# RWKV-5 attention followed by top-1 expert routing: own weights as column tiles, a scaling table held in PSUM, weights and routing steps moved

## The chip, the cores and the metric

The kernel runs on one core of one Trainium2 chip. The metric is the device time of one execution in microseconds (us). A core has five engines that run side by side and meet by semaphores: TensorE (PE; its weight loads are listed as PEld), VectorE (DVE), ScalarE (ACT), GpSimd (POOL) and SyncE (SP), which here only issues transfers. Transfers run on 16 DMA engines that the core's queues share.

## The reference

Two blocks follow each other. The first is RWKV-5 attention over r, k, v of batch 4, 8 heads, 768 steps and head size 48, with a decay w and a bonus u for each head and channel:

```python
for t in range(S):
    cur = np.einsum('bhd,bhe->bhde', u[None] * kt, vt)
    y[:, :, t] = np.einsum('bhd,bhde->bhe', rt, state + cur)
    state = w[None, :, :, None] * state + np.einsum('bhd,bhe->bhde', kt, vt)
```

Its output, 3072 tokens of 384 values, is the input of the second block, a switch layer with 8 experts of hidden size 1024. Each token goes to the expert with the largest logit:

```python
logits = x @ w_gate
expert_idx = np.argmax(logits, axis=1)
h = np.maximum(xe @ w1[e], 0.0)      # xe: the tokens of expert e
out[mask] = gate_w[mask, None] * (h @ w2[e])
```

All is float32. The step of u, by which a token weighs its own value, is a sum over 48 channels of r * k * u: one number for each token and head. It is called "own weight" below.

## The kernel before

The input decides between a path for usual decays, `fast()`, and a general one. These inputs take `fast()`, whose order of instructions on every engine is written out by hand (`manual_schedule`); nothing is planned by a scheduler there. Waits between engines are added by the framework.

**Attention: 32 units.** A unit is one batch, one half of the sequence (384 steps, 3 chunks of 128) and one pair of heads (hp, 0 to 3). The two heads of a pair lie on partitions 0 to 47 and 64 to 111; rows 48 to 63 and 112 to 127 of r and k are zero. Units run in the order batch, half, pair. For a unit:

- `load_rk`, `load_kt` and `load_v` bring r and k (two halves of 144 KB), k with tokens on partitions, and v (144 KB each). SP issues them five units ahead. SP's transfers take turns on eight semaphores, so each waits for the landing of the eighth before it.
- `u_scale_k` (POOL) makes RK = r * k (L518) and K = k * W2 (L519); `u_scale_r` (DVE) makes R = r * W1 (L514); `u_scale_g` (POOL) makes Kg (L524). W1 and W2 are tables of powers of w, one row of 128 for each pair, made by ACT with `scaled` (L468). The first two units are scaled on DVE by `u_scale_first`.
- `u_own` (L536) multiplies RK by u: for each chunk and head one matmul of 48 rows and 128 columns, with one result column, written behind the scores in the PSUM bank of that head (P0 or P1). `u_products` (L546) makes the scores, 128 by 128 for each chunk and head, in the same banks.
- `u_diagonal` (ACT) copies the own weights out as dv (L554) and writes them on the diagonal of A (L557). `u_mask` (DVE, L568) copies the scores below the diagonal over it.
- `u_state` sums k and v of each chunk on PE in the bank Gp (L582) and runs the state over the chunks on DVE (L587, L589).
- `u_out` multiplies the old state by R (L603) and v by A (L607), for one head in each half of the columns of the array, into one of two banks yp, which ACT copies out as y (L610).

In step u of the loop the engines get: the loads of unit u+5; the scalings of u+2; scores, state and mask of u+1; `u_out(u)`. Every fourth step aside, `u_gate` (L638) then turns a finished chunk of 128 tokens to rows and makes its 8 logits. PSUM has eight banks: two each for P0, P1 and y, one for Gp, one for gates.

**Weights.** `pieces` cuts the weights that the first experts need into transfers of 384 KB: w2 of experts 0 to 4 (`w2_load`, NW = 5), and w1 of the first two expert tiles. Three are issued before the loop; the others are spread over the steps that have no row stores. The w2 of experts 5 to 7 lies where attention keeps its own buffers, and is loaded as these come free.

**Routing.** For each batch, small DVE and ACT steps (`choose`) take the maximum, the chosen expert and its weight; `ranks` counts tokens for each expert with matmuls into a y bank, and `onehots` (L851) makes one-hot matrices of the ranks. The list `todo` spreads these steps and the stores of rows (L196) over the loop; what belongs to the fourth batch comes after it. `Routes.early` makes the lists of tokens of the first two expert tiles from the first two batches; `to_index` (L861 to L872) turns one-hot products into token indices.

**Experts.** 24 tiles of 128 tokens follow, then a tile of short segments that is woven in: `hidden` (L1078) multiplies w1 by the tokens, `product` (L1089) multiplies by w2, `weigh` and `store` write rows back. Tiles 0 and 1 use what was prepared early, so the last routing steps run on DVE beside them: `ranks`, `bases`, `order`, `slots`, `onehots`, and `index`, whose matmuls (L861) stand inside `t1.hidden`. Only then are the experts of tiles 2 and later known, and SP loads their w1 (L1031).

Of the kernel before, what the change touches and what calls it, by code (L numbers as in the profile page):

```python
# [10 lines left out]
FP32 = mybir.dt.float32  # L11
# [37 lines left out]
def bc(ap, shape):  # L49
    return ap.to_broadcast(shape)  # L50
# [3 lines left out]
def rwkv5_then_switch(ctx, tc, r, k, v, rk, tok, wu_in, wg, wgh, w1, w2, out):  # L54
# [18 lines left out]
    wu = consts.tile([128, 2, HP], FP32, name="wu")  # L73
# [156 lines left out]
    def general():  # L230
# [24 lines left out]

        ub = ca.tile([128, HP, 2], FP32, name="ub")
        nc.vector.memset(ub, 0.0)
        for hi in range(2):
            q = slice(64 * hi, 64 * hi + 64)
            nc.vector.tensor_copy(ub[q, :, hi], wu[q, 1, :])  # L260
# [39 lines left out]
        def half(b, hp, hf, kT, rT, vt, St, xb):  # L300
# [41 lines left out]
            for c in range(HC):  # L342
                if c < ns:
                    nc.tensor.matmul(dsp[:, c * 2 * D:(c + 1) * 2 * D], lhsT=Kt[:, c, :], rhs=vt[:, c0 + c, :],
                                     start=True, stop=True, skip_group_check=True)
                nc.tensor.matmul(dsp[:, nd + 2 * c:nd + 2 * c + 2], lhsT=RK[:, c * C:(c + 1) * C],
                                 rhs=ub[:, hp, :], start=True, stop=True, skip_group_check=True)
# [81 lines left out]
    def fast():  # L429
# [12 lines left out]
        with tc.manual_schedule():  # L442
            nc.gpsimd.tensor_tensor(RKs[0], rks[0][:, 0:HC * C], rks[0][:, HC * C:], op=ALU.mult)

# [13 lines left out]
        Gp = ps.tile([128, HC, 2, 64], FP32, name="Gp", tag="g", bufs=1)  # L458


        W1 = ca.tile([128, HP, C], FP32, name="W1")
# [8 lines left out]
        def tables(hp):  # L470
            scaled(W2, Wr, hp, w_64)
            scaled(W1, Wp, hp, w_64)

# [5 lines left out]

        def idle(n):  # L480

            warm = ps.tile([128, 128], FP32, name="warm", tag="y", bufs=2)
            for i in range(n):
                nc.tensor.matmul(warm, lhsT=ident, rhs=ident, start=True, stop=True, skip_group_check=True)
# [17 lines left out]
        def u_scale_first(u):  # L502

            x = units[u]
            hp = x["hp"]
            if u:
                nc.vector.tensor_tensor(x["RK"], x["r"], x["k"], op=ALU.mult)
            for o, i, tab in (("K", "k", Wr), ("R", "r", Wp)):
                nc.vector.scalar_tensor_tensor(out=x[o], in0=x[i], scalar=w_64[:, hp:hp + 1],
                                               in1=bc(tab[:, hp, None, :], [128, HC, C]), op0=ALU.mult, op1=ALU.mult)  # L510

        def u_scale_r(u):
            x = units[u]
            nc.vector.tensor_tensor(x["R"], x["r"], bc(W1[:, x["hp"], None, :], [128, HC, C]), op=ALU.mult)  # L514

        def u_scale_k(u):
            x = units[u]
            nc.gpsimd.tensor_tensor(x["RK"], x["r"], x["k"], op=ALU.mult)  # L518
            nc.gpsimd.tensor_tensor(x["K"], x["k"], bc(W2[:, x["hp"], None, :], [128, HC, C]), op=ALU.mult)  # L519
# [8 lines left out]
        def u_own(u):  # L528

            x = units[u]  # L530
            hp, P = x["hp"], x["P"]
            for c in range(HC):
                for hi in range(2):
                    q = slice(64 * hi, 64 * hi + D)
                    o = HC * C + c
                    nc.tensor.matmul(P[hi][:, o:o + 1], lhsT=x["RK"][q, c, :],  # L536
                                     rhs=wu[q, 1, hp:hp + 1], start=True, stop=True, skip_group_check=True)
# [11 lines left out]
        def u_diagonal(u):  # L549
            x = units[u]  # L550
            A, P = x["A"], x["P"]
            dv = ca.tile([128, 2, HC], FP32, name="dv", bufs=2)
            for hi in range(2):
                nc.scalar.copy(dv[:, hi], P[hi][:, HC * C:HC * C + HC])  # L554
            for hi in range(2):
                for c in range(HC):
                    nc.scalar.activation(A[:, hi, c, :], ident, func=ACT.Copy, scale=dv[:, hi, c:c + 1])  # L557

        def u_scores(u, parts=(u_own, u_products, u_diagonal)):
            units[u]["P"] = [ps.tile([128, 512], FP32, name=f"P{hi}", tag=f"P{hi}", bufs=2) for hi in range(2)]  # L560
            for part in parts:
                part(u)
# [31 lines left out]
        def u_out(u):  # L594

            x = units[u]
            yp = ps.tile([128, HC, C], FP32, name="yp", tag="y", bufs=2)
            for c in range(HC):
                old = x["St"][:, c - 1] if c else units[u - HP]["St"][:, HC - 1] if x["hf"] else None
                for hi in range(2):  # L600
                    q = slice(64 * hi, 64 * hi + 64)
                    if old is not None:
                        nc.tensor.matmul(yp[q, c, :], lhsT=old[:, hi, :], rhs=x["R"][:, c, :],  # L603
                                         start=True, stop=False, skip_group_check=True)
                for hi in range(2):
                    q = slice(64 * hi, 64 * hi + 64)
                    nc.tensor.matmul(yp[q, c, :], lhsT=vh(x, c, hi, 64), rhs=x["A"][:, hi, c, :],  # L607
                                     start=old is None, stop=True, skip_group_check=True)
            x["y"] = cy.tile([128, HC * C], FP32, name="y", tag="y", bufs=8)
            nc.scalar.copy(x["y"], yp.rearrange("p c t -> p (c t)"))  # L610
# [40 lines left out]
        stores = set()  # L651
        for b in range(B - 1):
            g = 2 * HP * (b + 1) + 2
            for i in range(3):
                todo[g + min(i, 1)].append(lambda b=b, i=i: chosen[b][i]())
            for i in range(3):
                todo[g + 1 + i].append(lambda b=b, i=i: chosen[b][3](i, 3))
                stores.add(g + 1 + i)
            for i, step in enumerate(R.ranks(b, "y") + R.onehots(b, 3)):
                todo[min(g + 2 + max(i - 1, 0), NU - 1)].append(step)  # L660
            if b == NB - 1:
                for step, i in zip(R.early("y"), (5, 6, 8, 11)):
                    todo[g + i].append(step)
# [3 lines left out]
        pieces = [lambda e=e, i=i: w2_load(e, q=slice(i, i + 1)) for e in range(NW) for i in range(FQ)]  # L667
        n = FQ * (NW - 1)
# [6 lines left out]
        with tc.manual_schedule():  # L675
# [8 lines left out]
            u_scores(0, (u_own, u_diagonal, u_products))  # L684
            tables(2)
            u_scale_first(1)
# [3 lines left out]
            u_mask(0)  # L690
            u_scores(1, (u_own, u_diagonal, u_products))
            u_scale_g(0)
            load_kt(4)
            u_scale_g(1)
            for hp in (3, 0, 1):
                tables(hp)
            u_state(0)
            u_scale_r(2)
            idle(2)
            for u in range(NU):  # L700
# [6 lines left out]
                if u == NU - 1:  # L707
                    w2_load(NW)
                if u + 2 < NU:
                    u_scale_k(u + 2)  # L710
                    if u:
                        u_scale_r(u + 2)
                    u_scale_g(u + 2)
                if u == 0:
                    u_out(0)
                    u_mask(1)
                    u_state(1)
                elif u + 1 < NU:
                    u_scores(u + 1)
                    u_state(u + 1)  # L720
                    u_mask(u + 1)
                if u:
                    u_out(u)
                if u == 2:
                    gate_columns()
# [27 lines left out]
            w2_load(E - 1)  # L753
# [14 lines left out]
            t2.load_w1(wp, FQ)  # L768
            t0.weigh(mo)
# [15 lines left out]
    class Routes:  # L785
# [15 lines left out]

        def begin(self):
# [6 lines left out]
        def ranks(self, b, tag):  # L809
# [4 lines left out]
            def product():  # L814
                nonlocal rp
                rp = self.ps.tile([128, G + 1, E], FP32, name="rkp", tag=tag, bufs=BUFS[tag])
# [40 lines left out]
        def to_index(self, pool, Bv, n, n_chunks, tag, nm):  # L857

            idp = self.ps.tile([128, 2, n], FP32, name="idp", tag=tag, bufs=BUFS[tag])
            for g in range(n_chunks):  # L860
                nc.tensor.matmul(idp.rearrange("p u j -> p (u j)"), lhsT=self.At[:, g, :],  # L861
                                 rhs=Bv[:, g].rearrange("p u j -> p (u j)"), start=g == 0, stop=g == n_chunks - 1)
            idl = pool.tile([128, 2, n], FP32, name=nm + "l")
            nc.vector.tensor_copy(idl, idp)
            emp = pool.tile([128, n], FP32, name=nm + "e")
            nc.vector.tensor_scalar(out=emp, in0=idl[:, 0, :], scalar1=0.0, scalar2=float(N + 128),
                                    op0=ALU.is_equal, op1=ALU.mult)
            raw = pool.tile([128, n], FP32, name=nm + "r")
            nc.vector.scalar_tensor_tensor(out=raw, in0=idl[:, 0, :], scalar=128.0, in1=idl[:, 1, :],
# [402 lines left out]
def _layout(name, *a):  # L1272
# [10 lines left out]
    elif name == 'w,u':  # L1283
        q = _np.stack([x.reshape(HP, 2, D).transpose(1, 2, 0) for x in a], axis=2)
        q = _np.concatenate([q] + [q[:, D - 1:]] * (64 - D), axis=1)
        a = q.reshape(128, 2, HP)
    else:
        a = a[0]
# [34 lines left out]
```

## Time and profile before

| | |
|---|---|
| median of 3 runs | 411.44 us (410.87 to 412.72) |
| profiled execution, own time | 410.42 us |
| its span, first to last instruction | 408.7 us |
| granted TensorE clock, mean | 0.989 |
| busy: PE, DVE, POOL, ACT | 394.4, 241.7, 150.1, 127.6 us |
| moved by DMA | 99.01 MB, mean 242 GB/s |
| L536 own, 384 matmul records | 26.6 us busy, 250 ns each |
| L514 R, 30 | 21.3 us busy, 709 ns each |
| L518 RK, 30 | 31.8 us busy, 1060 ns each |

A matmul of float32 stands in the trace as two pairs of weight load and matmul, so the 192 instructions of `u_own` are 384 records. Matmuls are pipelined: the mean of one is longer than the time between two. How long a group holds PE is read from the chain of work that ended last, in order of time. Busy shares are means over stages with different limits. A wait is put down to the semaphore event that came last by the profile; where the named engine had long been done, it was another, often a transfer. The trace also has the landing of each transfer as events of its semaphore.

### The profile page before, as it was taken

The numbers are of one execution on the slowest core, as the hardware profiler recorded it, in microseconds if no ns is written. First come the engines' busy times: TensorE is split into PE (matmuls) and PEld (weight loads), VectorE is DVE, ScalarE is ACT, GpSimd is POOL, SyncE is SP. The second block draws the span as 40 slices with busy tenths as digits, with TensorE's granted clock in tenths as the row PEclk, the third lists the DMA queues.
The fourth block names the chain that finished last, engine by engine and source line by source line (L and its number), as shares of the span: only waits on it lengthen the run. The fifth ranks groups of instructions, "written<-read, shape, count | busy, mean of one in ns | idle before, by whom it ended". The sixth has DMA issues, their size and how long they took to land.

```text
span 408.7 us, 10600 instructions
## 1 busy us (share of the span) xinstructions
PE 394.4 (96%) x3983; PEld 325.2 (80%) x3983; DVE 241.7 (59%) x800; ACT 127.6 (31%) x395; POOL 150.1 (37%) x194
## 2 busy tenths in 40 slices
PE   7999999999999999999999999999999999999980
PEld 7899999999999777788878777777778787777760
DVE  7886688889986834444884574646444444343400
ACT  3787777787674221111111011011111110110110
POOL 6898779668770021121111222121222111110100
PEclk9999999999999999999999999999999999999995
DMA  7999999999999959569967696977868675555001
GB/s 257 268 281 267 257 277 304 267 270 303 287 259 374 297 153 377 193 200 337 327 223 244 203 337 213 321 226 246 305 214 285 230 269 194 178 189 174 34 24 27
DMA packets 42995, 99.01 MB, mean 242 GB/s; under 512 B 5237, under 2 KB 16522, under 8 KB 42930
## 3 DMA queue, kind: packets, MB, share of 16 engines
q1 hardware_dynamic: 39072, 86.94, 66.4%
q0 software_dynamic: 3712, 11.23, 9.0%
q8 instruction: 36, 0.59, 0.7%
q14 instruction: 29, 0.24, 0.2%
q10 hardware_dynamic: 146, 0.01, 0.0%
HBM read 88.72 MB, written 9.65 MB: 241 GB/s over the span
## 4 chain that ended last, share of the span: by engine, by line
PE 94%; DMA 1%; SPq 1%; ACT 1%; POOL 0%; issue 0%; DVE 0%; POOLq 0%
PE hp L1078 32%; PE yp L1089 30%; PE P L536 6%; PE P L546 6%; PE yp L607 5%; PE yp L603 4%; PE rp L638 4%; PE Gp L582 3%; PE hg L1138 1%; PE yg L1155 1%; DMA w_all<-in_r_k_units_dram 1%; ACT A L557 0%; PE idp L861 0%; PE xTp L1059 0%; SPq L96 0%; SPq L108 0%
## 5 line engine op out<-in xcount | busy, mean ns | idle before, releaser
L1078 PEld LDWEIGHTS hp<-xT,w1s 128*128 128x128 f32 x1152 | 133.1, 192 | 10.4 <-issue 3.7
L1078 PE MATMUL hp<-xT,w1s 128*128 128x128 f32 x1152 | 135.2, 276 | 0.0
L1089 PE MATMUL yp<-w_all,hT 128*128 (+1 forms) x384 | 128.0, 486 | 0.0
L1089 PEld LDWEIGHTS yp<-w_all,hT 128*128 128x128 f32 x384 | 71.1, 190 | 44.2
L1080 ACT ACTIVATE hT<-hp 128x512 f32<-128x512 f32 x48 | 28.7, 598 | 217.9 <-PE hp L1078 189.8
L1009 DVE STREAM_TRANSPOSE xT<-xs 32x96 f32<-32x96 f32 x336 | 90.4, 269 | 5.1 <-DMA xs<-x_hbm,idx 0.2
L1100 POOL DMA_INDIRECT out_dram<-yo,idx x22 | 22.3, 1013 | 183.8 <-DVE yo L1093 175.6
L1093 DVE TENSOR_SCALAR yo<-yp,xs 128x384 f32<-128x384 f32 x22 | 13.6, 618 | 114.0 <-PE yp L1089 114.0
L557 ACT ACTIVATE A<-ident,dv 128x128 f32<-128x128 f32 x192 | 59.7, 389 | 0.2 <-ACT dv L554 0.2
L568 DVE COPY_PREDICATED A<-mask,P 128x384 f32<-128x384 int32 x64 | 36.6, 589 | 7.0 <-ACT A L557 6.3
L518 POOL TENSOR_TENSOR w_all<-w_all 128x384 f32<-128x384 f32 x30 | 31.8, 1060 | 21.3 <-PE yp L607 7.2
L607 PE MATMUL yp<-A,w_all 128*64 128x128 f32 x384 | 38.2, 274 | 0.0
L1053 POOL DMA_INDIRECT xs<-x_hbm,idx x22 | 21.3, 969 | 31.1 <-DVE oe L967 24.7
L603 PE MATMUL yp<-w_all,St 128*64 128x128 f32 x320 | 31.7, 274 | 0.0
L519 POOL TENSOR_TENSOR w_all<-w_all,W 128x384 f32<-128x384 f32 x30 | 30.8, 1027 | 0.0
L546 PE MATMUL P<-w_all 48*128 48x128 f32 x384 | 29.5, 286 | 0.5 <-ACT dv L554 0.5
L536 PEld LDWEIGHTS P<-wu,w_all 48*128 48x128 f32 x384 | 23.9, 187 | 4.3 <-issue 1.4
L536 PE MATMUL P<-wu,w_all 48*128 48x1 f32 x384 | 26.6, 250 | 0.2 <-DMA w_all<-in_r_k_units_dram 0.2
L524 POOL TENSOR_TENSOR Kg<-w_all,Wg 128x288 f32<-128x288 f32 (+1 forms) x32 | 25.0, 784 | 2.3 <-DVE Wg L478 2.3
L546 PEld LDWEIGHTS P<-w_all 48*128 48x128 f32 x384 | 24.2, 188 | 0.6 <-ACT dv L554 0.6
L607 PEld LDWEIGHTS yp<-A,w_all 128*64 128x64 f32 x384 | 24.1, 137 | 0.3 <-DVE A L568 0.2
L589 DVE SCALAR_TENSOR_TENSOR St<-St,pw,Gp 128x96 f32<-128x96 f32 x64 | 20.1, 314 | 4.1 <-PE Gp L582 2.2
(167 smaller groups left out, 286.2 us busy)
## 6 DMA issues: line engine op xcount, KB each, us to landing
w1s<-in_moe_w_dram SPq DMA_DIRECT2D x21, 1536.0 KB
wq<-in_moe_w_dram SPq DMA_DIRECT2D x32, 384.0 KB
w_all<-in_v_k_units_dram SPq DMA_DIRECT2D x64, 144.0 KB
w_all<-in_r_k_units_dram SPq DMA_DIRECT2D x56, 144.0 KB
w_all<-in_moe_w_dram SPq DMA_DIRECT2D x20, 384.0 KB
w1s<-in_moe_w_dram SPq DMA_DIRECT2D x12, 384.0 KB
w_all<-in_moe_w_dram SPq DMA_DIRECT2D x3, 1536.0 KB
x_hbm<-xb SPq DMA_DIRECT2D x9, 385.0 KB
```

The source lines that it names most:

```text
L518: nc.gpsimd.tensor_tensor(x["RK"], x["r"], x["k"], op=ALU.mult)
L519: nc.gpsimd.tensor_tensor(x["K"], x["k"], bc(W2[:, x["hp"], None, :], [128, HC, C]), op=ALU.mult)
L536: nc.tensor.matmul(P[hi][:, o:o + 1], lhsT=x["RK"][q, c, :], rhs=wu[q, 1, hp:hp + 1], start=True, stop=True, skip_group_check=True)
L546: nc.tensor.matmul(P[hi][:, c * C:(c + 1) * C], lhsT=x["K"][q, c, :], rhs=x["R"][q, c, :], start=True, stop=True, skip_group_check=True)
L557: nc.scalar.activation(A[:, hi, c, :], ident, func=ACT.Copy, scale=dv[:, hi, c:c + 1])
L568: nc.vector.copy_predicated(A[:, hi], bc(mask[:, None, :].bitcast(I32), [128, HC, C]), P[hi][:, 0:HC * C].rearrange("p (c t) -> p c t", t=C))
L603: nc.tensor.matmul(yp[q, c, :], lhsT=old[:, hi, :], rhs=x["R"][:, c, :], start=True, stop=False, skip_group_check=True)
L607: nc.tensor.matmul(yp[q, c, :], lhsT=vh(x, c, hi, 64), rhs=x["A"][:, hi, c, :], start=old is None, stop=True, skip_group_check=True)
L1009: nc.vector.transpose(out[d:d + 32, :, t:t + 32], x[t:t + 32, :, d:d + 32])
L1078: nc.tensor.matmul(p[:, f, :], lhsT=self.w1[:, q, d, o:o + 128], rhs=self.xT[:, d, :], start=d == 0, stop=d == DT - 1)
L1080: nc.scalar.activation(self.hT[:, 4 * fb:4 * fb + 4, :], p, func=ACT.Relu)
L1089: nc.tensor.matmul(p, lhsT=self.hT[:, f, :], rhs=rhs, start=f == 0, stop=f == FT - 1)
```

## The change

**Own weights.** u is laid out twice (`wu[:, 1:3]`), once for each head with zeros in the other's rows. One matmul then takes all 128 rows of RK, 64 tokens as columns, and has both heads as two result columns. Two such matmuls, for the two halves of a chunk's 128 tokens, are column tiles of the array. All own weights of a unit lie in P0, and dv is one copy.

**W1 in PSUM.** The table W1 of pair 0 and 1 lies in the last 128 columns of the two P1 banks, that of pair 2 and 3 in the last 128 of the two y banks. Those banks are now taken once and kept. The rank and index products of the routing go to the last 128 columns of the Gp bank.

**Start.** Products of unit 0 come ahead of own; RK of units 0 and 2 is made on DVE; the tables of pairs 2 and 3 come first, those of 0 and 1 after steps 1 and 2; `idle` is gone.

**Weights and routing.** `pieces` has w2 of experts 0 to 3. That of expert 4 is loaded where expert 7's was, after the stores of the last rows; that of expert 7 behind the w1 of tile 2. Routing steps and stores of a batch go one step later; two one-hot steps of the third batch no longer fit the loop and follow it as `rest`.

```diff
-    wu = consts.tile([128, 2, HP], FP32, name="wu")
+    wu = consts.tile([128, 3, HP], FP32, name="wu")
...
-        Gp = ps.tile([128, HC, 2, 64], FP32, name="Gp", tag="g", bufs=1)
-        W1 = ca.tile([128, HP, C], FP32, name="W1")
+        gb = ps.tile([128, 512], FP32, name="Gp", tag="g", bufs=1)
+        Gp = gb[:, 0:HC * C].rearrange("p (c h d) -> p c h d", c=HC, h=2)
+        small = gb[:, HC * C:]
+        Ps = [[ps.tile([128, 512], FP32, name=f"P{hi}", tag=f"P{hi}", bufs=2) for hi in range(2)] for i in range(2)]
+        ys = [ps.tile([128, 512], FP32, name="yp", tag="y", bufs=2) for i in range(2)]
+        W1 = [t[:, HC * C:] for t in (Ps[0][1], Ps[1][1], ys[0], ys[1])]
...
-            scaled(W1, Wp, hp, w_64)
+            nc.scalar.activation(W1[hp], Wp[:, hp, :], func=ACT.Copy, scale=w_64[:, hp:hp + 1])
...
-            nc.vector.tensor_tensor(x["R"], x["r"], bc(W1[:, x["hp"], None, :], [128, HC, C]), op=ALU.mult)
+            nc.vector.tensor_tensor(x["R"], x["r"], bc(W1[x["hp"]][:, None, :], [128, HC, C]), op=ALU.mult)
+
+        def u_rk(u, eng=nc.gpsimd):
+            x = units[u]
+            eng.tensor_tensor(x["RK"], x["r"], x["k"], op=ALU.mult)
 
         def u_scale_k(u):
             x = units[u]
-            nc.gpsimd.tensor_tensor(x["RK"], x["r"], x["k"], op=ALU.mult)
...
             for c in range(HC):
-                for hi in range(2):
-                    q = slice(64 * hi, 64 * hi + D)
-                    o = HC * C + c
-                    nc.tensor.matmul(P[hi][:, o:o + 1], lhsT=x["RK"][q, c, :],
-                                     rhs=wu[q, 1, hp:hp + 1], start=True, stop=True, skip_group_check=True)
+                o = HC * C + 2 * c
+                for t in (slice(0, 64), slice(64, 128)):
+                    nc.tensor.matmul(P[0][t, o:o + 2], lhsT=x["RK"][:, c, t], rhs=wu[:, 1:3, hp],
+                                     start=True, stop=True, skip_group_check=True)
...
-            dv = ca.tile([128, 2, HC], FP32, name="dv", bufs=2)
-            for hi in range(2):
-                nc.scalar.copy(dv[:, hi], P[hi][:, HC * C:HC * C + HC])
+            dv = ca.tile([128, HC, 2], FP32, name="dv", bufs=2)
+            nc.scalar.copy(dv, P[0][:, HC * C:HC * C + 2 * HC].rearrange("p (c h) -> p c h", h=2))
...
-            yp = ps.tile([128, HC, C], FP32, name="yp", tag="y", bufs=2)
+            yp = ys[u % 2][:, 0:HC * C].rearrange("p (c t) -> p c t", c=HC)
...
             for i in range(3):
-                todo[g + min(i, 1)].append(lambda b=b, i=i: chosen[b][i]())
+                todo[g + i].append(lambda b=b, i=i: chosen[b][i]())
             for i in range(3):
-                todo[g + 1 + i].append(lambda b=b, i=i: chosen[b][3](i, 3))
-                stores.add(g + 1 + i)
-            for i, step in enumerate(R.ranks(b, "y") + R.onehots(b, 3)):
-                todo[min(g + 2 + max(i - 1, 0), NU - 1)].append(step)
+                todo[g + 2 + i].append(lambda b=b, i=i: chosen[b][3](i, 3))
+                stores.add(g + 2 + i)
+            for i, step in zip((2, 3, 3, 4, 5, 6, 7), R.ranks(b, small) + R.onehots(b, 3), strict=True):
+                (todo[g + i] if g + i < NU else rest).append(step)
...
-        pieces = [lambda e=e, i=i: w2_load(e, q=slice(i, i + 1)) for e in range(NW) for i in range(FQ)]
-        n = FQ * (NW - 1)
+        pieces = [lambda e=e, i=i: w2_load(e, q=slice(i, i + 1)) for e in range(NW - 1) for i in range(FQ)]
+        n = FQ * (NW - 2)
...
-            u_scores(0, (u_own, u_diagonal, u_products))
             tables(2)
+            tables(3)
+            u_scores(0, (u_products, u_own, u_diagonal))
...
-            for hp in (3, 0, 1):
-                tables(hp)
             u_state(0)
+            u_scores(2, (u_own,))
+            u_scale_k(2)
             u_scale_r(2)
-            idle(2)
...
+                if u in (1, 2):
+                    tables(u - 1)
...
-            w2_load(E - 1)
+            for step in rest:
+                step()
+            w2_load(NW - 1)
             for step in ranks:
                 step()
...
             t2.load_w1(wp, FQ)
+            w2_load(E - 1)
```

## The prediction

> **What bounds the kernel now.** First the page's busy shares and its chain that ended last:
>
> ```profile
> PE 394.4 (96%) x3983; PEld 325.2 (80%) x3983; DVE 241.7 (59%) x800; ACT 127.6 (31%) x395; POOL 150.1 (37%) x194
> PE hp L1078 32%; PE yp L1089 30%; PE P L536 6%; PE P L546 6%; PE yp L607 5%; PE yp L603 4%; PE rp L638 4%; PE Gp L582 3%; PE hg L1138 1%; PE yg L1155 1%; DMA w_all<-in_r_k_units_dram 1%; ACT A L557 0%; PE idp L861 0%; PE xTp L1059 0%; SPq L96 0%; SPq L108 0%
> ```
>
> TensorE carries the whole chain. The attention stage ends near 127 us, the expert stage fills the rest. The change works on attention, so the next view is the busy time by stretches (columns: PE, PEld, DVE, ACT, POOL, granted clock, DMA share, GB/s):
>
> ```profile
> 20.00:40.00 20.00, 20.00 (x372) 18.36 (x370) 15.31 (x35) 16.04 (x58) 18.30 (x20) 1.00 1.02 276
> 60.00:80.00 20.00, 20.00 (x383) 18.70 (x380) 16.88 (x45) 15.18 (x55) 15.59 (x17) 1.00 1.00 286
> 100.00:120.00 20.00, 20.00 (x387) 18.53 (x387) 18.06 (x57) 14.98 (x56) 15.01 (x18) 1.00 0.99 284
> ```
>
> PE is full, but so are the 16 DMA engines (share 1.0 at 280 GB/s). Who is ahead? SyncE's own waits say that it issues when an older transfer lands, not when an engine frees a buffer; POOL's first product of a unit (L518, needs r and k) waits too:
>
> ```profile
> SPq L108 <- DMA w_all<-in_moe_w_dram: 11.2, 10, 2.0
> SPq L108 <- DMA w1s<-in_moe_w_dram: 4.2, 4, 1.4
> POOL w_all L518 <- PE yp L607: 7.2, 5, 2.4
> POOL w_all L518 <- PE yp L603: 5.1, 6, 1.3
> ```
>
> L518's releasers are named as PE lines that had long ended, a different one each time; the landing events of the trace settle it. For all of the units 11 to 31, L518 starts 0.16 to 0.46 us after the second half of that unit's r and k has landed, 0.16 in most. The last unit's halves land at 116.22 and 116.76; L518 starts at 116.93. TensorE uses it here (chain in order of time):
>
> ```profile
> 120.65 0.71 PE rp L638 x16
> 121.36 0.76 PE P L536 x12
> 122.12 0.78 PE P L546 x12
> 122.90 0.32 PE Gp L582 x8
> ```
>
> So own weights of unit 31 start 4.6 us after its data landed; L518 and L519 take 2.0 of that. TensorE walks about one unit behind a transfer queue that is itself full. That is the slack which a faster TensorE can use up.
>
> **What the Trainium skill says.** "TensorE: Matmul & The Clock Gate", section LDWEIGHTS: a weight load costs its columns at 1.2 per ns, whatever its rows: 107 ns for 128, 53 for 64. The trace agrees in slope: records of 187 ns (128 columns, L536), 137 (64, L607), 123 (48, L582), 0.8 ns a column. "TensorEngine Tiling (Array Packing)", Key Properties: column tiles load and multiply in parallel, changing the tiling mode drains the array. The trace agrees: Gp, 48-column pairs in column tiles, takes 0.40 us for 12 and 0.32 for 8, so 20 ns each and 0.16 once. "PSUM — Partial Sum Buffer", section on bank collisions: two engines must be kept apart by bank and quadrant, disjoint columns do not help. The trace shows that ordering: the copy of dv (L554) reads three columns that own wrote early, and still waits 22.7 us in all for the products in its bank. "VectorE: DVE Perf Modes", section "Two Vector instructions with no wait between them": with two SBUF tensor inputs the second is read through an interface shared with GpSimd. L514 took 0.54 to 0.56 us alone and 1.22 beside L519 (at 118.08).
>
> **The change part by part.** Sums are made against the profiled execution: span 408.7, own time 410.42, 1.0 below the median of the runs shown, 411.44.
>
> *Own weights (L536).* 12 load and multiply pairs a unit stay 12, but of 64 columns with 2 results in column tiles instead of 128 columns with 1 in row tiles. Before: 0.76 us a unit. After: 53/2 = 27 ns each, 0.32, and the drain stays one per direction since row products follow. Bounds: no overlap of the tiles gives 12 x 53 = 0.64; Gp's 20 ns gives 0.24. I take 0.33: 0.43 off a unit, 13.8 us over 32. This is on the chain.
>
> *ACT's dv copies,* two to one: 0.16 us off a unit, hidden under PE as ACT idles; nothing.
>
> *Tables W1 in PSUM.* L514 now has one SBUF input. From PSUM a copy of 384 (L478) took 0.56 and a masked copy 0.59, so 0.6 to 0.65 and no more 1.2; mean 0.71 before. DVE is at 83% in 20 to 120 us, it gets 2 us of room and no time. But the tables of hp 2 and 3 lie in the two y banks. The streams of the changed program show the price: for u = 0, 1 mod 4 the matmuls of u_out(u) wait until DVE has made R of unit u+2, which waits for r of u+2 to land. Before, u_out waited for its mask alone. Queued behind it on PE: the gate of that unit and own and products of u+2.
>
> *Start.* RK of unit 0 moves from POOL (1.68 us) to DVE (0.54), unit 2's too; two idle matmuls (0.64 us) go; two tables are made later. Perhaps 1 us on PE by unit 2; POOL and the queue then decide, so nothing is left of it.
>
> *Weights moved.* w2 of expert 4 (4 x 384 KB) leaves the attention queue. A piece moves the landings by 1.49 us (25 pieces between 14 and 117 us, 37.3 us). By the issue order, 22 pieces stand before unit 31's r and k now and 18 after, 20 and 17 before unit 30's. Stores go one turn later, their number before unit 31 stays 6.
>
> *What attention gains.* PE alone could be 13.8 early. Unit 30 (hp 2): r, k landed 112.09, less 3 x 1.49 = 107.6. Then 0.16 to start, 0.65 for R, 0.1 to signal, 6 x 0.22 for u_out, 0.71 gate, 0.33 own: products at 110.9. They stood at 118.23 (117.47 + 0.76), so 7.3 earlier; unit 31 can add 0.43, its own landing would allow 8. Gain about 7.6. If R takes 1.2, 7.1; if a piece is worth 1.0 us (384 KB at the 390 GB/s of 124 to 132 us), 6; if landings also speed up, up to 11.
>
> *What the expert head gives back.* (a) Two of the three one-hot steps of the third batch (L851, three in 1.10 us at 126.42, in idle time) now stand on DVE ahead of the last ranks: 0.75 us in a chain that runs without a gap to here:
>
> ```profile
> 141.47 0.95 DVE L851 TENSOR_TENSOR At<-iota_f,rl 128x768 bf16<-128x768 f32 x1
> 142.77 0.98 PEld L861 LDWEIGHTS <-At 128*128 128x128 bf16 x24
> ```
>
> At is ready at 142.42, PE comes at 142.77: 0.35 spare, so 0.4 lost (0 to 0.8). (b) Expert 4's weights take the place of expert 7's behind the row stores, and expert 7's 1.5 MB stand on SP's queue between the w1 of tile 2 and of tile 3. There the queue is full (same columns):
>
> ```profile
> 152.00:156.00 4.00, 4.00 (x34) 3.73 (x33) 2.89 (x11) 0.42 (x1) 1.95 (x2) 1.00 1.02 387
> 156.00:160.00 4.00, 4.00 (x27) 3.21 (x26) 2.15 (x8) 0.78 (x2) 0.04 (x1) 1.00 1.02 370
> 160.00:164.00 4.00, 4.00 (x19) 2.67 (x18) 0.63 (x2) 0.00 (x0) 0.00 (x0) 1.00 0.97 360
> ```
>
> Tile 3's w1 landed at 161.09 and its first product ran at 163.33: 2.2 us spare. 1.57 MB at 390 GB/s are 4.0, so PE waits 1.8 (0 to 3.5). Tile 4's w1 landed at 167.03 for 173.85 and stays covered. After that the tiles run at PE's 10.5 us as before.
>
> The rewritten index step has four DVE operations as before, and the ranks' products move to Gp's bank with the same instructions: nothing, covered by PE.
>
> Sum: 7.6 - 0.4 - 1.8 = 5.4. Profiled 405.0, median 406.0.
>
> **Rivals.**
> *A, the queue becomes the bound* (likeliest): 406.0. For it: L518 on the heels of the landings for 21 units, DMA share 1.0. Against: a share of 1.0 may hide some overlap.
> *B, landings come forward with PE,* all of the PE time counts: 13.8 - 2.2 = 11.6, 399.8. For it: SP also waits some 9 us on PE for buffers; large packets reach 390 GB/s later. Against: eight transfers always in flight, 5 to 8 us from issue to landing.
> *C, DVE becomes the bound and the kernel ends slower:* DVE now holds u_out for half the units. It has 83 us of work in 100, 3.1 us a unit of 3.7. If R from PSUM costs over 1.3 us (0.65 more than supposed), DVE needs 3.7, attention gains nothing and the head still loses 2.2: 413.6. Against: 0.56 to 0.59 for PSUM reads of this size.
> *D, the tiles of own don't overlap:* 0.64 a unit, 0.12 x 32 = 3.8 gained, minus 2.2: 409.8.
>
> **How the numbers follow.** A 0.72, B 0.09, C 0.09, D 0.10. A's own range, from 6.0 - 4 to 9 - 0.5, is 403 to 409.5. To leave out no more than 2 in 10 the range takes A and most of D, and leaves B's and C's centres out: 401.5 to 410.5. About 0.5% (2 us) is what a measurement of this kernel can tell from no change: below 409.4 counts as faster. A nearly all, B and part of D: 0.81; the rest of D and A's tail: 0.09; C and a little of D: 0.10.
>
> **What would show it.** Right: own at 0.3 to 0.4 us per 12 in the chain; PE no longer full in 20 to 120, with waits of u_out on DVE R and of own or products on POOL; L518's twin still 0.16 after landings; attention ending near 120; a PE wait near tile 3 of 1 to 3 us. Wrong: attention ending before 116 (B), R above 1 us or DVE above 95% (C), own above 0.6 (D), no wait before tile 3 (the sum 1.8 too low).

## The result: 4.5% slower

The changed kernel takes 434.45 us (median; 427.71 to 436.02), the kernel before took 412.08 on the same chip: ratio 1.045, interval 1.030 to 1.060. The ratio, here and below, leaves out executions that ran in a slower state (of after it takes 427.71 and 434.03), so it is not the ratio of the medians. The profiled execution of after took 434.03, its span 432.3, 23.6 more than before. The last output of attention's 32 units is followed by the turn of tile 0 (`xTp`), which ends at 147.37 instead of 127.44: 19.9 us of the loss lie in attention. From there to the end it is 284.9 instead of 281.3: 3.7 lie in the expert stage.

The busy shares and the chain that ended last, of after:

```profile
PE 398.5 (92%) x3979; PEld 330.1 (76%) x3979; DVE 245.0 (57%) x802; ACT 128.0 (30%) x363; POOL 144.2 (33%) x192
PE 80%; DVE 8%; ACT 3%; issue 2%; DMA 2%; POOL 1%; POOLq 0%; SPq 0%
```

TensorE carried 94% of the chain before; now DVE, ACT, transfers and issue hold 15% of it. The stretches say where (columns as before: PE, PEld, DVE, ACT, POOL, granted clock, DMA share, GB/s):

```profile
20.00:40.00 20.00, 18.67 (x373) 17.68 (x374) 13.98 (x35) 17.18 (x57) 16.79 (x20) 1.00 0.98 255
60.00:80.00 20.00, 17.18 (x321) 16.40 (x317) 15.72 (x40) 13.38 (x42) 13.76 (x15) 0.91 1.03 295
100.00:120.00 20.00, 14.47 (x236) 13.87 (x233) 15.91 (x37) 10.43 (x34) 9.75 (x11) 0.83 0.86 243
```

Until about 60 us the two kernels walk side by side (own weights of unit 17 start at 68.49, before at 69.14). Then PE is idle 2.8 to 5.5 us in 20, does 321 and 236 instructions where it did 383 and 387, and its granted clock falls. The queue is no longer full at the end. The waits of after over the span (in total, times, longest):

```profile
DVE lg L637 <- ACT xb L636: 22.4, 20, 3.4
...
PE yp L603 <- DVE w_all L509: 7.4, 4, 3.3
...
PEld yp L603 <- ACT A L553: 6.6, 4, 2.3
...
PE yp L599 <- DVE w_all L509: 5.6, 4, 2.2
```

L599 and L603 are the matmuls of `u_out`, L509 is R. Before, the only wait of `u_out` in the profile was one of 0.2 us for its mask. The chain in order of time shows one round of it:

```profile
65.86 0.46 ACT xb L636
...
66.35 0.19 DVE lg L637
...
66.62 0.90 DVE ri L850
...
68.38 0.54 DVE w_all L509
...
69.70 1.05 DVE A L564 x2
70.75 0.97 DVE At L861
71.72 0.48 DVE w_all L509
...
72.34 0.69 PE yp L603 x4
73.03 0.43 PE yp L599 x4
...
74.73 1.19 PE rp L634 x16
...
76.57 1.05 DVE At L861
77.62 0.47 DVE w_all L509
...
78.67 0.22 PE yp L599 x4
```

The second L509 is R of unit 18 (pair 2, its table in a y bank). Its r had landed at 66.25. It starts at 71.65 because DVE works in order: ahead of it stand the logit sum of a gate (L637), steps of the routing (L850, L861) and two masks, and the logit sum itself waits for PE's gate and ACT's copy. Only after R may `u_out(16)` write its y bank, after 1.9 us of idle PE. Then comes the next gate, and the loop goes round. Four matmuls of output take 0.43 us here, and 0.22 again from 78.67 on: half speed.

In the expert stage the chain of after reads

```profile
172.73 5.37 PE hp L1088 x48
...
178.73 1.76 issue
180.50 7.09 PE yp L1099 x16
```

The product of tile 2 waits 2.4 us and then takes 7.09 instead of 5.16. The w2 of expert 7, issued at 168.65, landed at 180.41; the product starts 0.09 us later.

### The profile page after: what moved, and what is told of

Read it like the earlier page. It is cut to its first block, busy times and chain, and to the rows that moved or that the text cites. A ratio compares the mean times of both kernels' runs of the same rounds, so it can differ in the third digit from the quotient of the medians.

```text
span 432.3 us, 10511 instructions
## 1 busy us (share of the span) xinstructions
PE 398.5 (92%) x3979; PEld 330.1 (76%) x3979; DVE 245.0 (57%) x802; ACT 128.0 (30%) x363; POOL 144.2 (33%) x192
## 4 chain that ended last, share of the span: by engine, by line
PE 80%; DVE 8%; ACT 3%; issue 2%; DMA 2%; POOL 1%; POOLq 0%; SPq 0%
PE hp L1088 30%; PE yp L1099 29%; PE yp L603 5%; PE yp L599 4%; PE rp L634 4%; PE P L543 3%; ACT A L553 2%; DVE w_all L509 2%; DVE At L861 1%; PE hg L1148 1%; PE yg L1165 1%; DVE A L564 1%; PE Gp L578 1%; PE P L533 1%; DMA w_all<-in_r_k_units_dram 1%
## 5 line engine op out<-in xcount | busy, mean ns | idle before, releaser
L1099 PE MATMUL yp<-w_all,hT 128*128 (+1 forms) x384 | 129.8, 491 | 2.4 <-issue 2.4
L603 PE MATMUL yp<-A,w_all 128*64 128x128 f32 x384 | 44.2, 305 | 9.6 <-DVE w_all L509 7.4
L599 PE MATMUL yp<-w_all,St 128*64 128x128 f32 x320 | 36.8, 305 | 8.4 <-DVE w_all L509 5.6
L513 POOL TENSOR_TENSOR w_all<-w_all 128x384 f32<-128x384 f32 x29 | 29.1, 1003 | 34.8 <-issue 14.2
L603 PEld LDWEIGHTS yp<-A,w_all 128*64 128x64 f32 x384 | 28.7, 155 | 10.5 <-ACT A L553 6.6
L543 PE MATMUL P<-w_all 48*128 48x128 f32 x384 | 31.1, 296 | 0.4 <-POOL Kg L522 0.2
L599 PEld LDWEIGHTS yp<-w_all,St 128*64 128x64 f32 x320 | 23.7, 155 | 8.9 <-ACT A L553 6.6
L522 POOL TENSOR_TENSOR Kg<-w_all,Wg 128x288 f32<-128x288 f32 (+1 forms) x32 | 22.8, 714 | 3.9 <-DVE Wg L473 3.1
L634 PE MATMUL rp<-IW,y 128*64 128x104 f32 x384 | 23.3, 269 | 0.0
```

The lines of the kernel that those rows point to most:

```text
L513: eng.tensor_tensor(x["RK"], x["r"], x["k"], op=ALU.mult)
L543: nc.tensor.matmul(P[hi][:, c * C:(c + 1) * C], lhsT=x["K"][q, c, :], rhs=x["R"][q, c, :], start=True, stop=True, skip_group_check=True)
L634: nc.tensor.matmul(rp[q, hp, :], lhsT=y[:, c * C + 64 * j:c * C + 64 * j + 64], rhs=IW[:, hp, :], start=True, stop=True, skip_group_check= ...
L1099: nc.tensor.matmul(p, lhsT=self.hT[:, f, :], rhs=rhs, start=f == 0, stop=f == FT - 1)
```

## The experiments

Times are medians of all executions; the kernel before was run beside each group (411.2 to 412.9). Every kernel computes the whole reference.

| run | us | ratio to before, 95% interval |
|---|---|---|
| after_swap | 410.96 | 0.998 (0.996 to 1.000) |
| after_sbuf_table | 412.77 | 1.000 (0.996 to 1.003) |
| after_w7_early | 426.36 | 1.026 (1.020 to 1.032) |
| after_swap_w7 | 406.97 | 0.988 (0.980 to 0.996) |
| before_own_tiles | 411.66 | 0.998 (0.996 to 1.001) |
| before_weights | 412.31 | 0.999 (0.996 to 1.002) |
| before_tables_in_y | 437.06 | 1.062 (1.055 to 1.068) |
| after_r_first | 418.82 | 1.018 (1.012 to 1.023) |
| swap_w7_r_first | 408.67 | 0.989 (0.981 to 0.997) |
| swap_old_weights | 409.96 | 0.994 (0.992 to 0.997) |
| swap_w7_old_routing | 406.31 | 0.983 (0.976 to 0.991) |
| swap_fill | 412.55 | 1.000 (0.996 to 1.003) |
| swap_fill_8 | 409.09 | 0.995 (0.992 to 0.997) |
| after_fill_waits | 437.97 | 1.060 (1.052 to 1.068) |
| after_fill_waits_0 | 426.79 | 1.038 (1.033 to 1.043) |

### Two tables change places

```diff
-        W1 = [t[:, HC * C:] for t in (Ps[0][1], Ps[1][1], ys[0], ys[1])]
+        W1 = [t[:, HC * C:] for t in (Ps[0][1], Ps[1][1], ys[1], ys[0])]
```

> The kernel after with one edit: the tables of pairs 2 and 3 change places in the two y banks, so that the vector engine's R of unit u+2 no longer reads the bank that the output of unit u writes. Instructions, sizes and queues stay as they are. Theory 1 (the bank couples u_out to R, and R stands behind the routing steps): the waits of L599 and L603 on L509 vanish, attention ends at 118 to 124 us instead of 147.4, time 402 to 410 us. Theory 2 (the routing steps spread over more units, or their results in Gp's bank, cause the stalls): no change, 428 to 436. Theory 3 (reading the table from PSUM at all is what costs): no change, 428 to 436.

23.5 us came back with two indices swapped. R of unit u+2 now reads the bank that `u_out(u+1)` writes, and that stands on PE behind the products of u+2, which need R anyway. So neither the routing steps, nor their results in Gp's bank, nor reading a table from PSUM made the loss. The forecast was still too low: 411, not 402 to 410.

The same with the tables back in SBUF:

```diff
-        W1 = [t[:, HC * C:] for t in (Ps[0][1], Ps[1][1], ys[0], ys[1])]
+        W1s = ca.tile([128, HP, C], FP32, name="W1")
+        W1 = [W1s[:, i, :] for i in range(HP)]
```

> The kernel after with all four tables for r in an SBUF tile, as in the kernel before; all else as after. Theory 1: 402 to 410 us, within 1% of the run with swapped banks, with L509 again over 1 us where it runs beside POOL's L517. Theory 2 (routing steps): 428 to 436. Theory 3 (reading from PSUM costs): 402 to 410 here, but 428 to 436 for the swapped banks.

Within 0.5% of the swap, as theory 1 had it, though again a little above its range. The table in PSUM is no handicap if its bank is the right one.

### The coupling alone, put into the kernel before

```diff
-            yp = ps.tile([128, HC, C], FP32, name="yp", tag="y", bufs=2)
+            yp = ys[u % 2][:, 0:HC * C].rearrange("p (c t) -> p c t", c=HC)
-        W1 = ca.tile([128, HP, C], FP32, name="W1")
+        W1 = [W1s[:, 0, :], W1s[:, 1, :], ys[0][:, HC * C:], ys[1][:, HC * C:]]
```

> The kernel before with the coupling alone: the tables of pairs 2 and 3 stand in the free ends of the y banks, each in the bank that the output of the unit two before reads and writes; the rank and index results move to Gp's bank to make room. Own weights, weights and start as before. Theory 1 (this coupling makes the loop): waits of the output's lines on the vector engine's R appear from about 60 us on, 420 to 435 us. Theory 2 (it takes the whole change, for instance TensorE running ahead of the queue): under 415 us.

437.06, as slow as the whole change and more. The run also moves the rank and index results to Gp's bank; the swap had them there too and lost nothing. In 10 to 150 us its output line L607 waits 8.3 us for R (L518 there) in three waits; one of them in order of time:

```profile
61.15 0.19 DVE L213 RECIPROCAL xb<-se 128x6 f32<-128x6 f32 x1
61.26 0.55 DVE L518 TENSOR_TENSOR w_all<-w_all,yp 128x384 f32<-128x384 f32 x1
...
61.96 0.44 PE L607 MATMUL yp<-w_all,St 128*64 128x128 f32 x4 [2.44 <-DVE w_all L518]
```

The last of a run of routing steps (L213), R, output: the coupling needs nothing else of the change. It is both sufficient (here) and necessary (the swap).

### R ahead of the routing steps

In the kernel after, `u_scale_r(u + 2)` moves to the head of step u, and `todo[u - 1]` behind it; DVE's instructions are the same.

> The kernel after, tables where it has them, but on the vector engine's queue each R goes ahead of the routing steps of the unit before; every instruction is kept. If the routing steps ahead of R make the loop: waits of L599 and L603's twins on R fall below 0.5 us each, attention ends at 120 to 128 us, 408 to 416 us (the wait before tile 2's product stays). If the bank order with the landing of r alone makes it: over 425 us.

418.82: 15.6 of the 22 us came back, a little less than expected. The order on DVE's queue, not the landing of r, is most of what held R. In the profiled execution, with 412.74 the fastest of six, 5 of the 9 idle stretches of PE over 0.7 us in attention remain, none over 1.4 us; L637 still stands ahead of R, and what makes up the rest was not taken apart further.

With the banks swapped, the same order gives nothing, since R is no longer wanted early:

> Swapped banks, early load of expert 7's w2, and each R ahead of the routing steps on the vector engine's queue. With the coupling gone R is wanted only by the products of its own unit, which wait for the landing of r and k anyway: within 2 us of the run without the new order (406.97). If R behind the routing steps still holds the products: 402 to 405 us.

### The load of expert 7

```diff
             w2_load(NW - 1)
+            w2_load(E - 1)
             for step in ranks:
...
-            w2_load(E - 1)
             t0.weigh(mo)
```

> The kernel after with one edit: the load of expert 7's w2 is issued right behind expert 4's, ahead of the w1 of tile 2 instead of behind it. Theory 1 (tile 2's product reads w2 at an index known at run time and so waits for the last of all w2 loads, 2.4 us, and its 16 products then run at a lower clock, 7.09 us instead of 5.16): the product of tile 2 starts without a wait and takes 5.2 us, time 3.5 to 4.5 us shorter than after. Rival (the wait comes from the w1 of tiles 2 and 3 in a full transfer queue): the wait stays or moves to tile 3, under 1.5 us gained.

The product of tile 2 starts without a wait and takes 5.16; from the end of attention to the end of the program it is 280.5 us instead of 284.9, 4.5 less. The medians differ by 8.1, more than expected; executions of this kernel lie between 421.31 and 430.95 and those of after between 427.71 and 436.02, so 4.5 is the better figure.

> Both edits, swapped banks and the early load of expert 7's w2. Theory 1: the two gains add, 398 to 406 us, faster than the kernel before by 1.5 to 3%. If the gains don't add, the early load only fills a wait that the swap moves elsewhere: within 1.5 us of the run with swapped banks alone.

The gains add: 406.97, 1.2% faster than the kernel before, and again a little above the expected range. This is the change as it might have been. Its stretch of 100 to 120 us, and its chain near the last unit:

```profile
100.00:120.00 20.00, 18.38 (x359) 16.85 (x357) 18.55 (x55) 14.98 (x51) 13.62 (x16) 1.00 0.91 256
```

```profile
109.04 3.30 DMA w_all<-in_v_k_units_dram
112.36 0.54 DVE w_all L509
...
113.85 0.45 PE P L533 x12
114.30 0.87 PE P L543 x12
...
116.81 0.71 PE rp L634 x16
117.52 0.30 PE P L533 x11
117.81 0.87 PE P L543 x12
```

Here the chain runs through a landing, R, own weights, products: near the last units the queue is part of the bound, and the clock stays at 1.00. Attention ends at 123.23, 4.2 before the kernel before.

### Own weights alone, weights alone

The first is the kernel before with `wu` of three rows, two heads in one product and one dv copy. The second has w2 of expert 4 out of attention, and the load of expert 7 behind it after the row stores.

> The kernel before with the own weights as column tiles alone (three rows of wu, both heads in one product, one dv copy); tables, weights, start and routing as before. If the transfer queue is the bound one unit ahead of TensorE, TensorE can only use up that lead: own and products of unit 31 could start 2.4 us earlier, 408 to 410 us, and SyncE's landings of r and k stay within 1 us of before. If TensorE's time counts in full, 32 x 0.3 us = 10 us: 401 to 403 us.

> The kernel before with the weights moved alone: expert 4's w2 leaves the attention stage and is loaded behind the row stores, with expert 7's behind it. TensorE has no idle time in attention before, so if TensorE is the bound there nothing is gained: 410 to 413 us, with r and k landing 3 to 5 us earlier by the last unit. If the queue alone is the bound: 405 to 408 us.

Neither gives a measurable gain alone, and for opposite reasons. With own weights alone PE runs into the queue (stretch 100 to 120 us, then a wait in 10 to 150 us):

```profile
100.00:120.00 20.00, 17.86 (x363) 16.27 (x359) 16.71 (x50) 13.44 (x46) 15.65 (x17) 1.00 1.03 282
```

```profile
PEld P L539 <- POOL w_all L513: 4.9, 10, 1.0
```

PE has 2.1 us of idle time in this stretch that it didn't have, and 8.0 from 20 us to the end of attention, where it had none; the queue is as full as before, and r and k of unit 31 land at 119.35 (before: 116.76), later than I had expected. With the weights alone, they land at 114.05, but PE is busy throughout and own weights of unit 31 start 6.35 us after RK is done instead of 3.36. My expectation for the first, 408 to 410, was a miss: the lead of one unit is not turned into time.

With swapped banks and the old weights:

> The kernel after with swapped banks, and the weights loaded as in the kernel before (expert 4's w2 in the attention stage, expert 7's behind the row stores). If the transfer queue is the bound of attention once TensorE is faster: attention ends 3 to 5 us later than with the weights moved, 409 to 412 us. If the own weights and the tables alone carry the gain: 405 to 408 us.

409.96, attention ends at 126.20, 3.0 later than with the weights moved. So with the old weights the gain is 0.6%, with the weights moved 1.2%. The ends of attention, one execution each, speak for the full gain taking both, a faster PE and a queue that lets it; by the times alone it is not shown, as the intervals overlap (0.992 to 0.997, 0.980 to 0.996).

### The spread of the routing steps

> Swapped banks, early load of expert 7's w2, and the routing steps and row stores at the units where the kernel before has them; the rank results stay in Gp's bank. If spreading the steps matters little once the coupling is gone: 405 to 409 us, within 2 us of the run without this edit. If the spread is worth something of its own: 409 to 413 us.

406.31 against 406.97: no difference that these runs can show. The spread neither costs nor pays once the coupling is gone.

### Is it the waits, or what follows them?

From 20 us to the end of attention PE is idle for 16.9 us in after and 0 before (sum of gaps over 0.05 us between its records; nine stretches of over 0.7 make 16.6 of it). As own weights take some 11 us less (below), 14 us of the loss of 19.9 must be something other than idle time. The record of the granted clock shows 0.5 for 23.9 us of this time (below, in the last section), in which PE is busy for 21.0: at half speed a loss of 10.5. The other 3 to 4 us were not taken apart; a part of them lies in the start, as own weights of unit 3 begin at 19.53 instead of 18.71.

Whether the wait lowers the speed can be tested. The first test is the wait before tile 2's product, with matmuls of no use put into it:

```diff
+            if j == 0:
+                warm = t.R.ps.tile([128, 128], FP32, name="warm", tag="rw", bufs=1)
+                for _ in range(26):
+                    nc.tensor.matmul(warm, lhsT=ident, rhs=ident, start=True, stop=True, skip_group_check=True)
             t.result(mo)
```

> The kernel after with swapped banks, w2 of expert 7 as late as in after, and 26 matmuls of the identity (128x128, about 2.9 us) put on TensorE ahead of the product of tile 2, where it waits for that load. Their results are not used. Clock theory (an idle TensorE of 2 to 3 us is answered by half the clock for the next 3 to 4 us): the 16 products take 5.2 to 5.5 us instead of 7.09 although the load is as late; time 1 to 2 us below the run with swapped banks (410.96). Rival (the product is slow because its operands arrive late): still about 7 us.

The product took 5.16 us, but the size was wrong: 26 float32 matmuls are 52 records and took 5.97 us. The load had landed at 157.69, and the product could only start at 161.9. So it cost 4.2 and gained 1.9. With 8 of them:

> As the run with 26 matmuls ahead of tile 2's product, with 8: 52 loads and multiplies took 5.97 us there, so these take 1.8 and end before the load of expert 7's w2 has landed. Clock theory (the product is slow because TensorE was idle for 2 to 3 us before): the wait that is left is about 1 us and the 16 products take 5.2 to 5.5 us instead of 7.09; time about 409 us, 1.5 to 2 below the run with swapped banks. Rival (slow because the operands landed just before): about 7 us, 411.

```profile
154.52 1.79 PE warm L1203 x16
156.31 0.07 issue
156.38 5.40 PE yp L1099 x16
```

The load landed at 156.29, as late as the product's start; yet the 16 products take 5.40, and the time is 1.9 below the swap alone (by medians; the intervals against the kernel before meet, 0.992 to 0.997 and 0.996 to 1.000). The wait is what lowers the speed, not the late operand.

In the loop of after, 8 such matmuls ahead of some `u_out`:

> The kernel after, tables where it has them, with 8 matmuls of the identity (128x122, about 1.8 us) ahead of the outputs of units 13, 17, 21, 25 and 29, those that wait for R; their results are not used. The waits for R stay as long as they are, counted from the same release. If the lower clock after each wait is a large part of the loss (10 us by the trace): the granted clock of 60 to 140 us rises from 0.75-0.91 to above 0.95 and the time falls by 5 to 10 us from 434.45. If the waits alone count: no change, or up to 3 us slower where the matmuls outlast a wait.

A miss of mine: I had counted the waiting units one too high, so the waits stayed (six of 1.0 to 2.7 us), the matmuls came as additional work, and the time was 437.97, not lower. Put ahead of units 12, 16, 20, 24 and 28:

> As the run with 8 matmuls ahead of the outputs of units 13 to 29, but ahead of those of units 12, 16, 20, 24 and 28: the trace of that run shows the long waits (1.6 to 2.7 us) in these, one unit before its matmuls, which therefore only added work. If the lower clock after each wait is a large part of the loss: idle time of TensorE in attention falls from 16.6 to below 9 us, matmuls behind the waits run at full speed, and the time falls by 4 to 9 us from 434.45. If the waits alone count: 433 to 437 us.

426.79, 7.7 us less than after by the medians. The intervals of the two overlap (1.033 to 1.043, 1.030 to 1.060), so the size rests on the profiled executions. The stretch of 60 to 140 us, first of after, then of this run:

```profile
60.00:140.00 80.00, 65.81 (x1134) 62.16 (x1130) 58.89 (x150) 46.28 (x149) 45.22 (x50) 0.85 0.72 205
```

```profile
60.00:140.00 80.00, 74.75 (x1387) 69.79 (x1386) 64.52 (x174) 52.10 (x165) 45.29 (x50) 1.00 0.84 240
```

The granted clock is 1.00 throughout, attention ends at 137.47 instead of 147.37. From 20 us on PE is idle for 6.9 us instead of 16.9, and the matmuls put in hold it for 10.0: the waits are as long as before, and the 9.9 us come from the clock. So in these executions about half of attention's loss is the serial loop, and half the slow matmuls behind its waits.

## Why the prediction was wrong

The forecast was 406.0 us; the sum failed in one step, and that step outweighs all others.

| step of the sum | forecast | measured |
|---|---|---|
| own weights, 32 units | -13.8 on PE | about -11 on PE |
| what attention gains | -7.6 | +19.9 (with swapped banks and early w2 of expert 7 -4.2) |
| two one-hot steps ahead of the index | +0.4 | 0 |
| expert 7's load | +1.8, at tile 3 | +2.4 wait and +1.9 slow, at tile 2 |

**The step that failed** is in "What attention gains": "Then 0.16 to start, 0.65 for R, 0.1 to signal, 6 x 0.22 for u_out". The prediction had found the coupling, and named what is queued behind the output, but priced R as if DVE were free when r lands. It asked how long R takes (0.54, better than assumed) and not what stands ahead of it. For R of unit 18, r had landed at 66.25 and R started at 71.65: 5.4 us where the sum had 0.16. Before the change this delay was harmless, as only the products of u+2 needed R. Once u_out(u) needs it too, PE's gate, ACT's copy, DVE's sum and routing steps, R and the next output form a ring. Two waits for R of 1.3 and 1.4 us stand at 28 and 56 us; the first longer one ends at 72.34, and the first one-hot step of the routing (L861, 70.65) stands right ahead of its R. The sum also had no term for the slower matmuls behind a wait, half of the loss.

**Rival C** had the place (DVE holds u_out for half of the units, ending slower) and the wrong price: it wanted R over 1.3 us or DVE over 95% busy. R took 0.54 and DVE was busy for at most 80% of those stretches. An engine far from full can still be the bound through the order of its queue. The rival's time of 413.6 was 21 us too low.

**Own weights** were priced nearly right. Behind a gate (L634, before L638), as for unit 31 in both kernels (0.30 + 0.87 above, 0.76 + 0.78 in the prediction), own and products take 1.17 us where they took 1.54: 0.37 less, not 0.43. Behind the few rank and index products it is 0.45 + 0.87, 0.22 less. That is about 11 us for 32 units. Own came as the sum had it; the products behind it take 0.09 longer, which the sum put at nothing. Whether that is the drain between column tiles and row tiles is not shown. The gain was not turned into time: with own weights alone it appeared as idle time of PE.

**The queue as the bound** was right. For units 11 to 19 RK (L513) still starts 0.15 to 0.22 us after its data landed, and own weights alone gave nothing. Four pieces fewer brought r and k of unit 31 from 116.76 to 113.19 in the best version, 0.9 us a piece instead of 1.49. From unit 20 on the queue was, but for unit 27, no longer what RK waited for: data of unit 24 landed at 86.64, RK started at 94.30, when own weights had freed its buffer.

**Expert 7's load** was priced at the wrong place. Tile 2's product picks its w2 by an index known at run time, so it waits for the last load into `w2_all`, whichever expert it needs: it starts 0.09 us behind that landing in after, and the wait is gone when the load comes early. The prediction looked only at the w1 behind it on the queue.

## What to carry to other kernels

Where waits go by the tile or bank, as in these kernels, a table that is written once is still a partner of whoever uses its PSUM bank: before putting it there, ask for each reader whose write must wait for it, and what stands ahead of that reader on its own in-order queue. Price a new wait by the time at which the releasing instruction can start there, not by its length. Short waits of TensorE can cost more than they last, so a wait that can't be removed may be worth filling with idle matmuls of the right size.

## What the runs showed of the hardware

**Half speed after a short wait.** Four weight loads of L599 took 0.48 us behind the wait that ended at 72.31 and 0.25 otherwise; the loads of tile 2's product 0.34 each instead of 0.19. The granted clock of after in these stretches:

```profile
66.00:72.00 6.00, 4.30 (x87) 3.87 (x84) 5.68 (x13) 4.67 (x16) 5.72 (x7) 1.00 1.03 295
72.00:76.00 4.00, 3.66 (x48) 3.69 (x48) 1.95 (x6) 0.60 (x3) 0.38 (x1) 0.57 1.03 310
76.00:80.00 4.00, 3.22 (x66) 2.99 (x65) 3.39 (x8) 2.87 (x9) 2.69 (x3) 1.00 1.07 301
```

In the trace's record of this clock every half-speed stretch, but for the one at the end of each execution, lasts one, two or three steps of 3.41 us, and all changes of an execution lie on one grid of that step. After 20 us, attention of after has 0.5 from 72.09 to 75.50, 89.15 to 92.57, 109.63 to 113.05, 116.46 to 119.87 and 130.11 to 140.35. PE's idle time within one step of the grid tells what follows better than the length of a gap. Over all 17 traces (after 20 us, the last 12 us left out), all 16 full-speed steps with 1.75 us or more of idle time were followed by a half-speed step, 12 of 39 with 0.93 to 1.74 were, and none of the 1806 with less. So the same gap need not have the same effect: one of 2.37 us in after_swap, cut by the grid into 1.09 and 1.27, kept full speed, while one of 1.93 in after, 1.79 of it in one step, did not. The Trainium skill, "TensorE: Matmul & The Clock Gate", Part 1, describes half rate after an idle window of about 3.4 us and says that this window runs freely. The steps and the grid agree with that; but here half of such a window idle was enough.

**R from PSUM was steady.** With its table in PSUM, R took 0.526 to 0.555 us in the 27 records of after from 15 to 130 us, many of them beside POOL; with it in SBUF 0.543 to 1.362 in the kernel before and 0.532 to 1.392 in after_sbuf_table, all those over 0.6 at least in part beside a multiplication on POOL. That gain is real; it had no use, as R was not what products waited for.
